# Windowed attention on one core: score tiles of 196 columns, sink keys inside a 68-key block, and no sink path of its own

## The chip, the cores and the metric

The kernel runs on one core of a Trainium2 chip. The core has a matmul engine (TensorE, PE in the tables, with its weight loads as PEld), a vector engine (VectorE, DVE), an activation engine (ScalarE, ACT), a general engine (GpSimd, POOL) and a sync engine that issues transfers (SyncE, SP). Each works through its own list of instructions in order and waits for others by semaphores. The metric is the device time of one launch in microseconds (us), the median of several runs; lower is better.

## The reference

Attention over 2 batches, 8 heads, 768 positions and 64 dimensions per head, with a causal window of 128 keys and 4 sink keys that every query sees; behind it two feed-forward networks without biases, all in float32.

```python
scores = scale * np.matmul(q, k.transpose(0, 1, 3, 2))
is_sink = pos[None, :] < int(n_sink)                 # n_sink 4
rel = pos[:, None] - pos[None, :]
keep = is_sink | ((rel >= 0) & (rel < int(window)))  # window 128
a = np.exp(np.where(keep, scores, -1e9) - rowmax)
x = (a / (a.sum(-1) + 1e-9)) @ v                     # heads side by side: 1536 x 512
x = ((x @ w1) * (x @ w2)) @ w3 @ w_out               # 512 -> 1024 -> 512
h = x @ w_in                                         # 512 -> 2048
out = softplus(h) @ w_out2                           # 2048 -> 512
```

## The kernel before, in words

Attention comes first, then stages 1 and 2 (the first network, with w3 and w_out multiplied ahead), stage 3 and stage 4 (the second network). The weights arrive as 64-bit numbers and are decoded on ACT and DVE; each matmul behind attention is three passes over split operands (`mm3`, L158 to L160). The decoding of the first weights of stage 1 (`D`) is planned among attention's work, that of the later ones is held behind `self.gate`, the last sink copy of attention on ACT (L463).

Attention works on pairs of heads, 8 pairs, each pair on the two halves of the partitions. A pair has six tiles of 128 queries. In a tile, queries are rows and keys are columns: 128 keys of the block before, the 4 sink keys, 128 keys of the own block, 260 in all (the first tile has its own block alone). Its upper 64 query rows need the first 196 columns, its lower 64 the last 196, except in tile 1, whose lower half takes all 260. `score` (L375) thus issues four matmuls a tile, one for each quarter of the array: half of the rows by head. `mask` (L383, DVE) scales, adds a bias and takes the row maximum, `exp` (L390, ACT) exponentiates and sums, `divide` (L404, POOL) scales by the inverse sum. `turn` (L416, PE) transposes the blocks of 128 keys, eleven a head in three groups g of up to four, into one of two PSUM buffers; `turned` copies them to SBUF on DVE (L426) or ACT (L428). `pv` (L451) multiplies with V: the weights are the 64 columns of V of a key block, the moving side is the turned block for the own tile and the tile behind it, so mostly 256 columns; two heads side by side in two column groups, in two PSUM banks.

The sinks of tiles 2 to 5 have a path of their own. `sink_copy` (L434, L435, L143, POOL) gathers their four columns of each tile, in a high and a low part, into a small tile for the pair; `sink_turn` (L460, PE) transposes it, `sink_turned` (L463, ACT) copies it, and `sink_pv` (L470, PE) adds four matmuls with the sink rows of V onto the banks. Those rows come by `sink_load` (L315) and are split by `sink_hi` (L140, POOL) and `sink_values` (L329, DVE). Then `x_hi` (L485, ACT) and `x_lo` (L143, DVE) write x for stage 1.

All steps are given to a planner (`Plan`) with engine, an assumed duration, what they need, and a rank (their place of adding plus an offset from `PUT_OFF`). It emits the steps in one order, which sets each engine's list; `form` adds a cost wherever PE changes its matmul form. 64 matmuls on a zero tile (`heat`, L510) fill PE at the start; four clears of the score banks (L515) are on DVE.

Of the kernel before, what the change touches and what calls it, by code (L numbers as in the profile page):

```python
# [28 lines left out]
KB = P + NSINK  # L29
EW = KB + P  # L30
# [17 lines left out]
    nw=-0.5, iota=-88.6, val=-119.97, inw=-95.56, cur=13.36, snk=-82.32, prev=-13.45, km1=109.48, m_1p=27.86,  # L48
    m_1c=141.05, km0=119.34, m_0=-213.7, m_p=-49.48, m_s=-4.31, m_c=11.17, heat=25.88, clear=(-245.94, -30.95),
    zeros=-0.98, q0=(204.36, 54.81), k0=(66.05, 234.03), v=(-1.12, -22.79), S=(19.74, 17.7), M=(-25.38, 3.94),  # L50
    E=(8.85, 10.07), N=(2.71, 10.01), RC=(-171.36, -209.28), C=(39.62, 36.0), T=(21.68, 18.7),
    P=(-267.36, -54.12), K=(-3.88, 41.33), PV=(21.75, 23.37), vs=-11.44, vsh=(39.09, -30.53),
    vsl=(-166.45, -4.22), KT=(21.93, 2.35), KC=(-167.02, -50.49), KV=(23.63, 24.74), XH=(-199.87, -147.15),
    XL=(1.84, 12.41), qk=(55.63, -83.58), flag=241.29, D=(12.72, 16.36),
)

PVS = ([(0, 0, 2), (1, 0, 2), (2, 0, 2), (3, 0, 1)], [(3, 1, 2), (4, 0, 2), (5, 0, 1)])


class Plan:  # L60
# [70 lines left out]
class Net:  # L131
# [116 lines left out]
    def mask_steps(self, pool):  # L248

        nc = self.nc  # L250
        n, w = self.val[:, 0:1], self.val[:, 1:2]
        rel = pool.tile([P, P], I32, name="rel")
        col = pool.tile([P, P], I32, name="col")
        inw, cur, snk, prev, k0, k1, self.m_0 = (
            pool.tile([P, P], F32, name=x) for x in ("inw", "cur", "snk", "prev", "k0", "k1", "m_0")
        )
        m_1, m_mid = self.m_1, self.m_mid = [pool.tile([P, EW], F32, name=x) for x in ("m_1", "m_mid")]

        def bias(engine, dst, keep):
            engine.tensor_scalar(out=dst, in0=keep, scalar1=-1.0, scalar2=MASKED, op0=ALU.add, op1=ALU.mult)  # L260

        def start():
            nc.gpsimd.iota(rel, pattern=[[-1, P]], base=0, channel_multiplier=1)
            nc.gpsimd.iota(col, pattern=[[1, P]], base=0, channel_multiplier=0)
            nc.gpsimd.memset(m_1[:, P:KB], -MASKED)

        return [
            ("iota", "Pool", 650, start, ()),
            ("val", "DVE", 550, lambda: self.window_values(pool), ()),
            ("inw", "DVE", 196, lambda: nc.vector.tensor_scalar(  # L270
                out=inw, in0=rel, scalar1=w, scalar2=None, op0=ALU.is_lt), ("iota", "val")),
            ("cur", "DVE", 202, lambda: nc.vector.scalar_tensor_tensor(
                out=cur, in0=rel, scalar=0.0, in1=inw, op0=ALU.is_ge, op1=ALU.mult), ("inw",)),
            ("snk", "DVE", 196, lambda: nc.vector.tensor_scalar(
                out=snk, in0=col, scalar1=n, scalar2=None, op0=ALU.is_lt), ("val", "iota")),
            ("prev", "DVE", 196, lambda: nc.vector.tensor_scalar(
                out=prev, in0=rel, scalar1=float(P), scalar2=w, op0=ALU.add, op1=ALU.is_lt), ("val", "iota")),
            ("km1", "DVE", 202, lambda: nc.vector.tensor_tensor(out=k1, in0=prev, in1=snk, op=ALU.max), ("prev", "snk")),
            ("m_1p", "Pool", 268, lambda: bias(nc.gpsimd, m_1[:, 0:P], k1), ("km1",)),
            ("m_1c", "DVE", 135, lambda: bias(nc.vector, m_1[:, KB:EW], cur), ("cur",)),  # L280
            ("km0", "DVE", 202, lambda: nc.vector.tensor_tensor(out=k0, in0=cur, in1=snk, op=ALU.max), ("cur", "snk")),
            ("m_0", "DVE", 135, lambda: bias(nc.vector, self.m_0, k0), ("km0",)),
            ("m_p", "Pool", 268, lambda: bias(nc.gpsimd, m_mid[:, 0:P], prev), ("prev",)),
            ("m_s", "Pool", 164, lambda: bias(nc.gpsimd, m_mid[:, P:KB], snk[:, 0:NSINK]), ("snk",)),
            ("m_c", "ACT", 160, lambda: nc.scalar.copy(m_mid[:, KB:EW], m_1[:, KB:EW]), ("m_1c",)),
        ]
# [14 lines left out]
    def sink_zeros(self, pool):  # L301
        nc = self.nc
        self.skb = []
        for i in range(2):
            t = pool.tile([P, QT - 2, 32], FR, name=f"sk{i}")
            d = pool.tile([P, P], FR, name=f"skd{i}")
            nc.gpsimd.memset(t.bitcast(F32), 0.0)
            self.skb.append((t, d))

    def sink_load(self, pool):  # L310
        self.part = pool.tile([P, 1], F32, name="part")
        self.vsraw = []
        for j in range(2):
            self.vsraw.append(self.ring.tile([P, B * NPAIR, P], F32, tag="u", name=f"vsraw{j}", bufs=5))
            self.nc.sync.dma_start(out=self.vsraw[j], in_=self.vsink[:, j])  # L315
        self.nc.sync.dma_start(out=self.part, in_=self.vpart)
        self.vshi, self.vs = [], []

    def sink_hi(self, pairs, j):
        if len(self.vshi) == j:  # L320
            self.vshi.append(self.ring.tile([P, B * NPAIR, P], FR, tag="u", name=f"vshi{j}", bufs=5))
        self.hi_pool(self.vshi[j][:, pairs], self.vsraw[j][:, pairs])

    def sink_values(self, pool, pairs, j):


        if len(self.vs) == j:
            self.vs.append(pool.tile([P, B * NPAIR, P], FR, name=f"vs{j}"))
        self.nc.vector.scalar_tensor_tensor(  # L329
            out=self.vs[j][:, pairs], in0=self.vshi[j][:, pairs].bitcast(F32), scalar=self.part[:, 0:1],  # L330
            in1=self.vsraw[j][:, pairs],
            op0=ALU.mult, op1=ALU.add,
        )

    def attention(self, pool, psum):
# [5 lines left out]
        shape = dict(qk=[P, S + QT * KB], v=[P, QT, P], e=[P, QT, EW], st=[P, 3, QT], pt=[P, 2 * QT - 1, P])  # L341
# [11 lines left out]
        def load_qk(pair, cuts=((0, S + QT * KB),)):  # L353
            for a, b in cuts:
                nc.sync.dma_start(out=buf("qk", pair)[:, a:b], in_=self.qk[pair][:, a:b])

        def load_v(pair):
            nc.sync.dma_start(out=buf("v", pair), in_=self.v[pair])

        def tile_columns(i):  # L360
            return slice(KB, EW) if i == 0 else slice(0, EW)

        def score(pair, i):

            qk, k = buf("qk", pair), S + (i - 1) * KB
            for par in range(2):
                held["S", 2 * pair + par, i] = banks[2 * (scores.index((pair, i)) % 2) + par]
            for half in range(2):

                rows = slice(half * D, half * D + D)  # L370
                a, b = (0 if i < 2 else D, EW) if half else (0, EW - D)
                a = a if i else KB
                for par in range(2):
                    r = slice(par * D, par * D + D)
                    nc.tensor.matmul(  # L375
                        held["S", 2 * pair + par, i][rows, a:b], qk[r, i * P + half * D : i * P + half * D + D],
                        qk[r, k + a : k + b], start=True, stop=True, skip_group_check=True,
                    )
# [33 lines left out]
        def turn(h, g):  # L412
            held["PT", h, g] = ps = psum.tile([P, 4, P], F32, tag="PT", name=f"ptp{h}_{g}", bufs=2)
# [8 lines left out]
        def turned(h, g):  # L422
            lo, n = max(4 * g - 1, 0), len(blocks(g))
            dst, src = buf("pt", h)[:, lo : lo + n, :], held.pop(("PT", h, g))[:, 0:n, :]
            if on_dve(h, g):
                nc.vector.tensor_copy(dst, src)  # L426
            else:
                nc.scalar.copy(dst, src)  # L428

        def sink_copy(h):  # L430
            sk = self.skb[(h // 2) % 2][0]
            src = buf("e", h)[:, 2:QT, P:KB]
            c = [slice((2 * g + h % 2) * NSINK, (2 * g + h % 2 + 1) * NSINK) for g in range(3)]
# [567 lines left out]
```

## Time and profile before

| what | value |
|---|---|
| runs | 590.69, 593.15, 593.74 us; median 593.15 |
| profiled execution | 593.03 us, span 591.1 us, 8685 instructions |
| busy, share of span | PE 98%, weight loads 79%, DVE 75%, ACT 60%, POOL 15% |
| bytes moved | 52.10 MB, HBM read 48.32, written 3.15 |

The time of an execution is its span, from the first to the last instruction, and some 1.9 us around it. Busy time is a union over an engine's instructions; matmuls are pipelined, so several records of PE overlap, and a busy PE may still be draining. Every fp32 matmul shows as two records and two weight loads. A group is named by its line, so the lines above tell which step it is.

### The profile page before, as it was taken

To read this page: it belongs to the slowest core of one execution; us is meant where nothing else is said; L and a number is where in the kernel's file an instruction comes from. 1 tells how busy PE (TensorE), PEld (TensorE's weight loads), DVE (VectorE), ACT (ScalarE), POOL (GpSimd) and SP (SyncE) were. 2 spreads that over 40 slices of the span, in tenths; PEclk is the share of its full clock that TensorE was granted. 3 is DMA by queue.
4 is the path that set the end of the run, shared out by engine and by line. 5 is a ranking of instruction groups with operands and counts; after the bars stand their busy time and mean duration, and the time that the engine had idled before them with its cause. 6 is when DMAs were issued, how large, how long until landed. Compare 5 with 4: busy or idle time off the path is not lost.

```text
span 591.1 us, 8685 instructions
## 1 busy us (share of the span) xinstructions
PE 579.9 (98%) x3096; PEld 468.1 (79%) x3096; DVE 441.9 (75%) x920; ACT 353.2 (60%) x720; POOL 90.9 (15%) x213
## 2 busy tenths in 40 slices
PE   8899999999999999999999999999999999999996
PEld 6576678888878878888888788888888888888884
DVE  7899969989998987784999799855545544644553
ACT  6899967667666565553566777643543444444352
POOL 3887840000000000000000111101110110111010
PEclk9999999999999999999999999999999999999998
DMA  8853204435453452441545031000100000100002
GB/s 261 302 172 106 63 2 145 160 123 177 145 171 113 144 160 89 142 132 31 165 137 178 2 120 59 0 1 0 73 0 1 1 1 1 71 0 1 1 0 78
DMA packets 15459, 52.10 MB, mean 88 GB/s; under 512 B 1968, under 2 KB 2480, under 8 KB 15408
## 3 DMA queue, kind: packets, MB, share of 16 engines
q1 hardware_dynamic: 15120, 50.95, 26.3%
q8 instruction: 26, 0.43, 0.3%
q10 hardware_dynamic: 288, 0.52, 0.2%
q14 instruction: 25, 0.20, 0.1%
HBM read 48.32 MB, written 3.15 MB: 87 GB/s over the span
## 4 chain that ended last, share of the span: by engine, by line
PE 63%; DVE 7%; ACT 6%; DMA 6%; issue 0%; POOL 0%; ACTq 0%; SPq 0%; DVEq 0%
PE h L160 7%; PE h L158 7%; PE h L159 7%; DMA raw_w<-w3t 4%; PE ox L158 4%; PE ox L160 4%; PE x2p L159 4%; PE x2p L158 4%; PE o L158 4%; PE o L160 4%; PE ox L159 4%; PE o L159 4%; PE x2p L160 4%; PE ab L160 3%; PE ab L159 3%; PE ab L158 3%
## 5 line engine op out<-in xcount | busy, mean ns | idle before, releaser
L736 POOL TENSOR_SCALAR spu<-spa 128x512 f32<-128x512 f32 (+1 forms) x49 | 30.3, 619 | 465.6 <-ACT spa L735 465.6
L143 DVE TENSOR_TENSOR gl<-spl,gh 128x512 fp32r<-128x512 f32 x47 | 32.6, 693 | 77.1 <-ACT gh L750 76.9
L734 ACT ACTIVATE spa<-h 128x512 f32<-128x512 f32 (+1 forms) x49 | 28.8, 588 | 88.8 <-PE h L160 88.6
L160 PE MATMUL ab<-x,u_w 128*128 128x512 f32 x192 | 75.0, 391 | 0.4 <-DVE u_w L143 0.3
L158 PE MATMUL ab<-x,u_w 128*128 128x512 f32 x192 | 75.1, 391 | 0.0
L159 PE MATMUL ab<-x,u_w 128*128 128x512 f32 x192 | 74.7, 389 | 0.0
L158 PE MATMUL h<-y,w4h 128*128 128x512 f32 x192 | 74.7, 389 | 0.0
L160 PE MATMUL h<-y,w4l 128*128 128x512 f32 x192 | 74.7, 389 | 0.0
L159 PE MATMUL h<-y,w4h 128*128 128x512 f32 x192 | 74.7, 389 | 0.0
L184 ACT ACTIVATE dt_w<-raw_w 128x512 bf16<-128x512 bf16 x64 | 42.4, 670 | 49.4 <-DMA raw_w<-w4d 13.8
L192 DVE SCALAR_TENSOR_TENSOR dc_w<-raw_w,dt_w 128x512 uint16<-128x512 uint16 x64 | 43.8, 689 | 14.5 <-ACT dt_w L187 13.4
L404 POOL TENSOR_SCALAR e<-e,st 128x260 f32<-128x260 f32 (+1 forms) x96 | 47.2, 510 | 16.5 <-ACT e L390 8.6
L390 ACT ACTIVATE e<-e,st 128x260 f32<-128x260 f32 (+1 forms) x96 | 46.5, 491 | 2.7 <-DVE st L383 2.5
L741 DVE SCALAR_TENSOR_TENSOR spu<-spu,spa 128x512 f32<-128x512 f32 (+1 forms) x49 | 33.3, 680 | 17.7 <-ACT spl L739 17.6
L187 ACT ACTIVATE dt_w<-dt_w,rebias 128x512 uint16<-128x512 uint16 x64 | 45.8, 722 | 1.2
L160 PEld LDWEIGHTS ab<-x,u_w 128*128 128x128 f32 x192 | 36.0, 188 | 8.6 <-DVE u_w L143 1.3
L158 PEld LDWEIGHTS ab<-x,u_w 128*128 128x128 f32 x192 | 36.1, 188 | 8.0 <-ACT u_w L216 0.6
L160 PEld LDWEIGHTS h<-y,w4l 128*128 128x128 f32 x192 | 36.1, 188 | 7.6
L159 PEld LDWEIGHTS h<-y,w4h 128*128 128x128 f32 x192 | 36.0, 188 | 7.5
L158 PEld LDWEIGHTS h<-y,w4h 128*128 128x128 f32 x192 | 36.0, 188 | 7.4
L159 PEld LDWEIGHTS ab<-x,u_w 128*128 128x128 f32 x192 | 36.0, 188 | 7.3
L739 ACT ACTIVATE spl<-spu 128x512 f32<-128x512 f32 (+1 forms) x49 | 30.4, 623 | 18.8 <-POOL spu L736 18.1
(138 smaller groups left out, 1335.3 us busy)
## 6 DMA issues: line engine op xcount, KB each, us to landing
raw_w<-w4d SPq DMA_DIRECT2D x32, 511.8 KB, 4.1
raw_w<-w SPq DMA_DIRECT2D x16, 511.8 KB, 4.3
raw_w<-w3t SPq DMA_DIRECT2D x16, 511.8 KB, 3.8
qk<-qk SPq DMA_DIRECT2D x7, 780.0 KB, 6.4
raw_wo<-wod SPq DMA_DIRECT2D x8, 511.8 KB, 3.7
v<-v SPq DMA_DIRECT2D x8, 384.0 KB, 5.6
out<-os SPq DMA_DIRECT2D x10, 256.0 KB, 2.3
vsraw<-vsink SPq DMA_DIRECT2D x2, 512.0 KB, 7.9
```

The costliest lines, as they stand in the source:

```text
L143: return engine.tensor_tensor(out=lo, in0=x, in1=hi.bitcast(F32), op=ALU.subtract)
L158: nc.tensor.matmul(ps, lhs[0], rhs[0], start=start, stop=False)
L159: nc.tensor.matmul(ps, lhs[0], rhs[1], start=False, stop=False)
L160: nc.tensor.matmul(ps, lhs[1], rhs[0], start=False, stop=stop)
L184: return nc.scalar.activation(t.bitcast(BF), x["top"].bitcast(BF), AF.Abs)
L187: return nc.scalar.activation(x["t"], x["t"], AF.Relu, bias=self.rebias[:, 0:1], scale=8.0)
L192: nc.vector.scalar_tensor_tensor(out=c, in0=x["top"], scalar=0x8000, in1=t, op0=ALU.bitwise_and, op1=ALU.bitwise_or)
L390: nc.scalar.activation(e, e, AF.Exp, bias=st[:, 0, i : i + 1], scale=-1.0, accum_out=st[:, 1, i : i + 1])
L404: nc.gpsimd.tensor_scalar(out=e, in0=e, scalar1=buf("st", h)[:, 2, i : i + 1], scalar2=1.0, op0=ALU.mult, op1=ALU.mult)
L736: nc.gpsimd.tensor_scalar(out=u[:, c], in0=a[:, c], scalar1=1.0, scalar2=1.0, op0=ALU.add, op1=ALU.mult)
L739: nc.scalar.activation(l[:, c], u[:, c], AF.Ln)
L741: nc.vector.scalar_tensor_tensor(out=u[:, c], in0=u[:, c], scalar=1.0, in1=a[:, c], op0=ALU.subtract, op1=ALU.subtract)
```

## The change

A strip is 64 queries, and keys are kept in blocks of 64, each with the four sink keys ahead of it (68 columns). A tile now has 196 columns: 68 of one single block and 128 of a pair of blocks. For the upper strip the pair is the 128 keys behind and the single block its own; for the lower strip the pair is the tile's own 128 keys and the single block the one two strips back. So each strip sees its 192 keys and the sinks in 196 columns, and every row of the tile uses all of them. `score` issues eight matmuls a tile, four of 68 columns and four of 128. `turn` turns the 68 columns to 68 rows, in which the sinks are the first four. `pv` multiplies the pair's block with V as before, for the strips that use it, and each single block with 68 rows of V, sinks among them, which a second transfer brings (`vu`, ten blocks of 68 rows a pair of heads). The sink path is gone: POOL's copies, the turn, the copy and the product, the load and the splits. The gate is now the last copy of `turned` on ACT. The first 16 of the warm-up matmuls write the banks and the turn buffers, in place of the clears. The masks are built by other steps, and the planner's offsets are new.

```diff
 def load_v(pair):
-    nc.sync.dma_start(out=buf("v", pair), in_=self.v[pair])
+    nc.sync.dma_start(out=buf("v", pair)[:, 0:QT], in_=self.v[pair])
+    nc.sync.dma_start(out=buf("v", pair)[0:KU, QT:], in_=self.vu[pair])
...
 def score(pair, i):
-    for half in range(2):
-        rows = slice(half * D, half * D + D)
-        a, b = (0 if i < 2 else D, EW) if half else (0, EW - D)
-        a = a if i else KB
-        for par in range(2):
-            r = slice(par * D, par * D + D)
-            nc.tensor.matmul(
-                held["S", 2 * pair + par, i][rows, a:b], qk[r, i * P + half * D : i * P + half * D + D],
-                qk[r, k + a : k + b], start=True, stop=True, skip_group_check=True,
-            )
+    for part in range(1 if i else 0, -1, -1):
+        for half in range(2):
+            s, rows = 2 * i + half, slice(half * U, half * U + U)
+            for par in range(2):
+                ...
+                if part:
+                    out, k = out[rows, 0:KU], k[:, s - 2 if half else s]
+                else:
+                    b = i if half or not i else i - 1
+                    out, k = out[rows, KU:EW], k[:, 2 * b : 2 * b + 2, NSINK:]
+                nc.tensor.matmul(
+                    out, qk[r, s * U : s * U + U], k, start=True, stop=True, skip_group_check=True
+                )
...
 def turn(h, g):
-    for j, (t, own) in enumerate(blocks(g)):
-        c = slice(KB, EW) if own else slice(0, P)
-        nc.tensor.transpose(ps[:, j, :], buf("e", h)[:, t, c], self.ident)
+    for j, (t, pair) in enumerate(blocks(g)):
+        n, c = (P, slice(KU, EW)) if pair else (KU, slice(0, KU))
+        nc.tensor.transpose(ps[0:n, j, :], buf("e", h)[:, t, c], self.ident)
...
-PVS = ([(0, 0, 2), (1, 0, 2), (2, 0, 2), (3, 0, 1)], [(3, 1, 2), (4, 0, 2), (5, 0, 1)])
+PVS = (
+    [(0, 0, 1), (0, 1, 3), (1, 3, 5), (2, 5, 7), (3, 7, 8)],
+    [(3, 8, 9), (4, 9, 11), (5, 11, 12)],
+)
...
 def pv(pair, bank):
-    for n, (j, s0, s1) in enumerate(PVS[bank]):
+    todo = [(slice(0, P), v[:, j], s0, s1, 1) for j, s0, s1 in PVS[bank]]
+    todo += [
+        (slice(0, KU), v[0:KU, QT + s - 2], s, s + 1, 0)
+        for s in range(8 if bank else 2, 12 if bank else 8)
+    ]
+    for n, (rows, w, s0, s1, own) in enumerate(todo):
...
-                nc.scalar.copy(dst, src)
+                self.gate = (nc.scalar.copy(dst, src),)
...
-        def sink_copy(h):
-        def sink_turn(pair):
-        def sink_turned(pair):
-        def sink_pv(pair):
```

PE's list, a stretch of the middle pairs, before (s are the scores, ptp the turns, xt the product with V, and with skd and vs the sink product):

```order
L375 MATMUL s_108<-qk_735 64x196
L416 MATMUL ptp_1_1086<-ident,e_850 128x128 x4
L416 MATMUL ptp_2_1094<-ident,e_850 128x128 x4
L470 MATMUL xt_0_1007<-skd_139,vs_437 128x128
L470 MATMUL xt_1_1040<-skd_139,vs_437 128x128
L470 MATMUL xt_0_1007<-skd_139,vs_439 128x128
L470 MATMUL xt_1_1040<-skd_139,vs_439 128x128
L375 MATMUL s_109<-qk_735 64x196
```

The sink product stands between turns and scores, as a form of its own (64 rows by 128 columns of the array). And PE's list after the change, from the end of a product with V on (pt are the turns):

```order
L448 MATMUL xt_1_983<-pt_843,v_605 64x64
L412 MATMUL pt_106<-ident,e_763 128x128
L412 MATMUL pt_106<-ident,e_763 68x128
L412 MATMUL pt_106<-ident,e_763 128x128
L412 MATMUL pt_107<-ident,e_763 68x128
L412 MATMUL pt_107<-ident,e_763 128x128
L412 MATMUL pt_107<-ident,e_763 68x128
L412 MATMUL pt_107<-ident,e_763 128x128
L371 MATMUL s_102<-qk_550 64x68
```

No sink product or turn stands between the others. Over two pairs of heads PE's list before (47.44 to 65.14 us of its trace) has 19 groups of one kind of matmul: three of products with V, seven of scores, seven of turns (a sink turn counted with its neighbours) and two sink products. After, a pair in the middle has seven: turns, scores, turns, scores, turns, scores, product; each score group covers two tiles.

DVE's list at the start, where the masks are built, before (m are the finished masks):

```order
L272 SCALAR_TENSOR_TENSOR cur<-rel,inw 128x128
L278 TENSOR_TENSOR k_102<-prev,snk 128x128
L281 TENSOR_TENSOR k_101<-cur,snk 128x128
L260 TENSOR_SCALAR m_103<-k_101 128x128
L260 TENSOR_SCALAR m_104<-cur 128x128
```

Here the two masks wait for nothing but DVE's own steps. DVE's list at the same place after the change:

```order
L275 SCALAR_TENSOR_TENSOR keep<-rel,inw 128x192
L272 TENSOR_SCALAR inw<-rel,val 128x128
L275 SCALAR_TENSOR_TENSOR keep<-rel,inw 128x128
L290 SCALAR_TENSOR_TENSOR m_100<-keep,bias 64x4
L284 TENSOR_TENSOR keep<-keep 128x4
L287 TENSOR_SCALAR bias<-keep 128x128
L378 ISA e_194,st_195<-s_103,bias 128x128
```

The second tile's mask, m_100, is finished on DVE (L290) from ACT's copy of a bias that POOL makes, and it stands ahead of the first tile's mask (L287) and the first masking (L378).

ACT's list at the end of attention, before (L428 are copies of turns, L463 the sink copy, L184 the first step of decoding):

```order
L428 COPY pt_1319<-ptp_0_1315 128x384
L485 CAST x_2_77<-xt_0_1283 128x256
L485 CAST x_2_81<-xt_0_1283 128x256
L485 CAST x_2_81<-xt_1_1304 128x256
L428 COPY pt_1342<-ptp_0_1338 128x384
L428 COPY pt_1342<-ptp_1_1349 128x512
L463 CAST skd_142<-skp_1385 128x128
L184 ACTIVATE dt_w_1_0_1420<-raw_w_1_0_1418 128x512
```

The first decoding step stands right behind the last sink copy. ACT's list there after the change:

```order
L424 COPY pt_1468<-pt_106 128x384
L424 COPY pt_1468<-pt_107 128x512
L463 CAST x_2_81<-xt_1_1478 128x256
L424 COPY pt_1500<-pt_106 128x384
L184 ACTIVATE dt_w_1_0_1578<-raw_w_1_0_1576 128x512
```

Decoding follows the last copy of a turn instead of the sink copy.

## Rows read from the trace of the kernel before

**Rows 1.** The page: busy us, share and instructions; PE's granted clock in tenths, 40 slices.
```profile
PE 579.9 (98%) x3096; PEld 468.1 (79%) x3096; DVE 441.9 (75%) x920; ACT 353.2 (60%) x720; POOL 90.9 (15%) x213
...
PEclk9999999999999999999999999999999999999998
```
**Rows 2.** Stretches: length, busy of PE, PEld, DVE, ACT, POOL, PE clock, DMA share, GB/s.
```profile
30.00:50.00 20.00, 19.87 (x234) 13.69 (x230) 19.79 (x81) 19.44 (x70) 16.11 (x38) 1.00 0.55 182
...
84.00:591.00 507.00, 500.89 (x2204) 412.83 (x2202) 369.90 (x617) 282.64 (x469) 30.31 (x49) 1.00 0.23 76
```
**Rows 3.** Timeline of PE: start and length in us, engine, line, tiles, form, count.
```profile
44.48 0.56 PE L375 MATMUL s<-qk 64*64 64x196 f32 x8
...
47.44 2.60 PE L451 MATMUL xt<-pt,v 128*64 128x256 f32 x28
...
51.82 0.44 PE L470 MATMUL xt<-skd,vs 64*128 64x128 f32 x4
52.19 0.89 PE L375 MATMUL s<-qk 64*64 64x196 f32 x16
...
60.76 1.09 PE L416 MATMUL ptp<-ident,e 128*128 128x128 f32 x8
61.78 0.44 PE L470 MATMUL xt<-skd,vs 64*128 64x128 f32 x4
...
64.44 0.65 PE L416 MATMUL ptp<-ident,e 128*128 128x128 f32 x4
64.93 0.27 PE L460 MATMUL skp<-ident,sk 128*128 128x128 f32 x1
65.14 0.65 PE L451 MATMUL xt<-pt,v 128*64 128x256 f32 x4
```
**Rows 4.** Timeline of PE's weight loads, with idle time before them and its releaser.
```profile
62.88 0.31 PEld L416 LDWEIGHTS ptp<-ident,e 128*128 128x128 f32 x3 [0.46 <-POOL e L404]
```
**Rows 5.** Waits of PE from 84 us on: us in total, times, longest.
```profile
PE ab L160 <- DVE u_w L143: 0.3, 1, 0.3
```
**Rows 6.** Timeline of PE, 10 to 20 us: the second run of warm-up matmuls.
```profile
11.82 1.18 PE L510 MATMUL heat<-idle 128*128 128x128 bf16 x18
```
**Rows 7.** Groups by line and shape (three of 30 to 84 us, one of 0 to 120): busy, mean ns.
```profile
L390 ACT ACTIVATE e<-e,st 128x260 f32<-128x260 f32 x51 | 25.7, 511 | 1.8 <-DVE st L383 1.8
L383 DVE CUSTOM_DVE_ANT_0 e<-s,m_mid 128x260 f32<-128x260 f32 x40 | 15.4, 416 | 0.1
...
L390 ACT ACTIVATE e<-e,st 128x128 f32<-128x128 f32 x10 | 4.0, 400 | 0.0
...
L383 DVE CUSTOM_DVE_ANT_0 e<-s,m 128x128 f32<-128x128 f32 x10 | 2.7, 274 | 0.0
...
L329 DVE SCALAR_TENSOR_TENSOR vs<-vshi,part,vsraw 128x384 fp32r<-128x384 f32 x4 | 2.7, 712 | 0.0
```
**Rows 8.** Timeline of ACT: the first decoding step, and the last sink copy.
```profile
24.23 0.69 ACT L184 ACTIVATE dt_w<-raw_w 128x512 bf16<-128x512 bf16 x1 [1.81 <-DMA raw_w<-w]
...
82.46 0.27 ACT L463 CAST skd<-skp 128x128 fp32r<-128x128 f32 x1 [2.73 <-PE skp L460]
```
**Rows 9.** Waits of PE, 12 to 30 us.
```profile
PE ptp L416 <- ACT pt L428: 1.4, 1, 1.4
```
**Rows 10.** Transfers by issue: queue, count, KB each, median us to landing.
```profile
qk<-qk SPq DMA_DIRECT2D x7, 780.0 KB, 6.4
...
v<-v SPq DMA_DIRECT2D x8, 384.0 KB, 5.6
...
vsraw<-vsink SPq DMA_DIRECT2D x2, 512.0 KB, 7.9
```
**Rows 11.** Timeline of all engines at the first masks.
```profile
4.04 0.67 POOL L260 TENSOR_SCALAR m_mid<-prev 128x128 f32<-128x128 f32 x1 [1.95 <-DVE prev L276]
...
5.63 0.29 DVE L383 CUSTOM_DVE_ANT_0 e<-s,m 128x128 f32<-128x128 f32 x1 [0.69 <-PE s L375]
```
**Rows 12.** Timeline of PE at the end of attention.
```profile
83.69 0.50 PE L158 MATMUL ab<-x,u_w 128*128 128x512 f32 x1
```

More of the change, by code (lines that the diff above doesn't have):

```diff
@@ L76, in form @@
     def form(s):
-        return {"S": "quarters", "KV": "rows", "PV": "columns"}.get(s["key"][0], "whole")
+        return {"S": "quarters", "PV": "columns"}.get(s["key"][0], "whole")
     def __init__(self, rings):
@@ new lines, in mask_steps, with behind @@
+        self.m_1 = pool.tile([P, EW], F32, name="m_1")
+        self.m_mid, self.m_0 = bias[:, 0:EW], bias[:, EW:]
+        snk, first = keep[:, 0:NSINK], keep[:, EW : EW + NSINK]
+        def start():
+            nc.gpsimd.iota(rel[:, EW - NSINK :], pattern=[[-1, P]], base=0, channel_multiplier=1)
+            nc.gpsimd.iota(col, pattern=[[1, NSINK]], base=0, channel_multiplier=0)
+        def behind():
+            for half, (own, pair) in enumerate(((0, 2 * U), (2 * U, U))):
+                r = slice(half * U, half * U + U)
+                nc.gpsimd.iota(rel[r, 0:U], pattern=[[-1, U]], base=own, channel_multiplier=1)
+                nc.gpsimd.iota(rel[r, U : EW - NSINK], pattern=[[-1, P]], base=pair, channel_multiplier=1)
@@ new lines, in inside, with kept, sinks, added @@
+        def inside(c):
+            nc.vector.tensor_scalar(out=inw[:, c], in0=rel[:, c], scalar1=w, scalar2=None, op0=ALU.is_lt)
+        def kept(c):
+            nc.vector.scalar_tensor_tensor(
+                out=keep[:, c.start + NSINK : c.stop + NSINK], in0=rel[:, c], scalar=0.0, in1=inw[:, c],
+                op0=ALU.is_ge, op1=ALU.mult,
+            )
+        def sinks():
+            nc.vector.tensor_scalar(out=snk, in0=col, scalar1=n, scalar2=None, op0=ALU.is_lt)
+        def added():
+            nc.vector.tensor_tensor(out=first, in0=first, in1=snk, op=ALU.max)
@@ L267, in mask_steps, with biased, second @@
+        def biased(engine, c):
+            engine.tensor_scalar(out=bias[:, c], in0=keep[:, c], scalar1=-1.0, scalar2=MASKED, op0=ALU.add, op1=ALU.mult)
+        def second():
+            nc.vector.scalar_tensor_tensor(
+                out=self.m_1[0:U, KU : KU + NSINK], in0=snk[0:U], scalar=-MASKED, in1=self.m_mid[0:U, KU : KU + NSINK],
+                op0=ALU.mult, op1=ALU.add,
+            )
+        mid, own = slice(0, EW - NSINK), slice(EW - NSINK, EW - NSINK + P)
         return [
-            ("iota", "Pool", 650, start, ()),
+            ("iota", "Pool", 500, start, ()),
+            ("iotb", "Pool", 900, behind, ()),
@@ L282, in mask_steps @@
[L282 to L285, printed above, removed]
+            ("inw", "DVE", 196, lambda: inside(own), ("iota", "val")),
+            ("cur", "DVE", 202, lambda: kept(own), ("inw",)),
@@ new lines, in mask_steps @@
+            ("snk", "DVE", 80, sinks, ("val", "iota")),
+            ("km0", "DVE", 80, added, ("cur", "snk")),
+            ("m_0", "DVE", 135, lambda: biased(nc.vector, slice(EW, EW + P)), ("km0",)),
+            ("inb", "DVE", 264, lambda: inside(mid), ("iotb", "val")),
+            ("prev", "DVE", 270, lambda: kept(mid), ("inb",)),
+            ("m_p", "Pool", 410, lambda: biased(nc.gpsimd, slice(0, EW)), ("prev", "snk")),
+            ("m_c", "ACT", 210, lambda: nc.scalar.copy(self.m_1, self.m_mid), ("m_p",)),
@@ L286, in mask_steps @@
+            ("m_1", "DVE", 80, second, ("m_c",)),
         ]
@@ L507, in attention, with warm @@
         heat = psum.tile([P, CH], F32, tag="X0", name="heat", bufs=1)
+        banks = [psum.tile([P, EW], F32, tag="S", name=f"s{i}", bufs=4) for i in range(4)]
+        held["turns"] = [psum.tile([P, 4, P], F32, tag="PT", name=f"pt{i}", bufs=2) for i in range(2)]
+        clear = [x for i in range(4) for x in (banks[i][:, 0:P], banks[i][:, P:EW])]
+        clear += [x[:, j, :] for x in held["turns"] for j in range(4)]
+        heats = clear + [heat[:, 0:P]] * (64 - len(clear))
+        def warm(i):
+            nc.tensor.matmul(heats[i], self.idle, self.idle[:, 0 : heats[i].shape[-1]], start=True, stop=True)
         for i in range(64):
             add(
-                "heat", "PE", 54, lambda i: nc.tensor.matmul(heat[:, 0:P], self.idle, self.idle, start=True, stop=True),
-                i, after=() if i < 44 else [("M", 0, 5)],
-            )
-        banks = [psum.tile([P, EW], F32, tag="S", name=f"s{i}", bufs=4) for i in range(4)]
-        for i in range(4):
-            add("clear", "DVE", 330, lambda i: nc.vector.memset(banks[i], 0.0), i)
-        add("zeros", "Pool", 1200, lambda: self.sink_zeros(pool))
+                "heat", "PE", 54, warm, i, after=() if i < 44 else [("M", 0, 5)],
+            )
         for j in range(2):
```

185 lines of the change are left out of this document (51 added, 134 removed).

## The prediction, made before the changed kernel ran

> **What bounds the kernel now.** [...] A busy PE need not be the bound, since PE counts as busy while a matmul drains; so next come the stretches [rows 2]. From 84 us on PE is busy 500.9 of 507 us: there the stages behind attention stream 512-column matmuls, which the change doesn't touch. The change lives in the first 84 us, where all engines are nearly full: from 30 to 50 us PE is busy 19.87, VectorE (DVE) 19.79, ScalarE (ACT) 19.44 and GpSimd (POOL) 16.11 of 20 us [rows 2]. Which sets the pace is seen in PE's list over two pairs of heads, 47.44 to 65.14 us [rows 3]: each group starts as the one before it drains. Only once in this stretch is the load row idle for longer than at every change of matmul form: 0.46 us at 62.88, for POOL [rows 4]. After 84 us PE's waits sum to 0.3 us [rows 5]. So from about 30 us on attention runs at the pace of PE's own list, 17.70 us for two pairs, and what leaves this list moves the end, as far as the other engines follow.
>
> **PE's prices** [rows 3]. Every fp32 matmul runs as two passes. A score group of two 196-column tiles (x16) lasts 0.89 us, one of a single such tile (x8) 0.56; a tile is thus 0.33: two passes of 196 columns with the four quadrants at once, 0.84 ns a column. Turns: x8 lasts 1.09, x4 0.65, so a 128-column step costs 0.11, with its own 128-column weight load inside it. The product with V (x28, 2.60 us) is 14 steps, two heads side by side: 1408 columns a head, twice, at 0.84 are 2.37, the rest is start and drain. A group has a fixed price: from 60.76 to 61.78 eight turns take 1.02, of which 8 x 0.109 is 0.87, so 0.15.
>
> **The change, per pair of heads.**
> - Sink product (L470): 51.82 to 52.19, -0.37, its change of form included.
> - Sink turn (L460): 64.93 to 65.14 where the form changes behind it, 0.21, and one step, 0.11, where more turns follow: -0.17.
> - Other groups: two pairs hold 19, two of them sink products. In the new order the same work repeats seven groups a pair: turns, scores of two tiles, turns, two tiles, turns, two tiles of which one is the narrow first, product. That is 14 for two pairs where 17 stood: three fewer at 0.15, -0.23 a pair.
> - Scores: 196 columns as 68 and 128. The one tile with 260 columns on a half now has 196: 64 x 2 x 0.84, -0.11. Five tiles get two more starts at about 3 ns (0.109 less 128 x 0.84 is 2): +0.03.
> - Product with V: the columns stay, the steps grow from 14 to 36, of which 28 have 64 columns. No row shows a long run of 64-column steps. From below such a step costs its columns, 0.054; from above as much as a 128-column step, 0.109. Nearest is the idle warm-up: 18 bf16 matmuls, each with a weight load of its own, in 1.18 us [rows 6]; less some 0.23 for the last one's latency that is 0.056 a step. I take 0.057, with 22 more starts: +0.08. The upper end adds 28 x 0.052 = 1.46, and ten 68-column waves of the scores another 0.5.
>
> Sum: -0.37 - 0.17 - 0.23 - 0.08 + 0.08 = **-0.77 us a pair**.
>
> [...]
>
> **Do the others follow?** Per pair DVE runs ten masks of 260 columns at 416 ns, against 274 for 128 [rows 7]: 1.08 ns a column, 64 columns fewer, -0.69. ACT: 511 against 400, ten times 0.054, and a sink copy of 0.27 goes [rows 8]: -0.8, as much as PE. POOL had 3.9 of 20 us to spare [rows 2] and loses 64 columns of each division and six sink copies. DVE shrinks by 0.08 less than PE, and in its fullest 20 us it had 0.21 to spare, where the decoding of the next stage's weights lies beside attention. It should just follow; I count no gain beyond PE's.
>
> **The start** is not PE's. ACT stands still for 1.81 us until 24.23, waiting for the first weights of the next stage [rows 8], and PE then waits 1.4 us for ACT's copy [rows 9]. The bytes ahead of these weights hardly change: four query-key loads of 780 KB, three V loads of 384 and the sink values, 1024, are 5296 KB [rows 10]; now 792 KB each, 384 + 340 (68 rows of 5 KB), no sink values: 5340. SP issues two DMAs for each V load, and the second V load now stands ahead of the fourth query-key load; three sink issues go. The first masks lose: on DVE the second tile's mask (L290) waits for ACT's copy of POOL's bias, and the first tile's mask and all that follows is queued behind it. The first masking starts at 5.63 now [rows 11]; POOL's bias took 0.67 for 128 columns, and a copy and two handovers lie behind it, so I expect about 6. ACT still reaches the weights earlier, by some twenty exponentials at 0.054, and then waits longer. Of the first two pairs' 1.54 us I count half, with none and all as ends. DVE and POOL also lose the splits of the sink values (six each; DVE's took 0.71 us for 384 columns [rows 7]) and the clearing of banks and buffers, which 16 of the warm-up matmuls take over. All of it lies before 31 us, where ACT's stall and PE's wait for ACT cover it: I count nothing, and the full gain of the start, the upper end, is what it could be worth.
>
> **The tail.** Four matmuls of the next stage ran between the last turns; two do now. Each is 0.23 us (507 us for 2204 [rows 2]): +0.45. Behind attention PE's list is the same row for row. Decoding of the next weights was released by the last sink copy, at 82.46 [rows 8]; now by ACT's last turn copy, ahead of the last product, so it should lead PE by more.
>
> Sum: six pairs at -0.77 are -4.6, the start -0.77, the tail +0.45: **-4.9 us**. The profiled execution took 593.03 us (span 591.1 and 1.9 around it), the median of the runs 593.15. Predicted: 588.1 us.
>
> **Rivals.**
> 1. *Narrow steps don't hide their loads: slower.* A 64- or 68-column step costs what a 128-column one does: 38 x 0.052 = +1.98 us a pair, net +1.21; times 8, +0.45: 603 us. It decides from 20 ns a step on (0.77 / 38), a step of 0.075. For it: no long run of 64-column steps has a row. Against: turns and warm-up hide loads that are as long as their streams. [...] Chance 0.07.
> 2. *More than forecast.* The start gains in full and the shorter chain from exponential to turn takes PE's wait of 1.4 [rows 9] and half of the 0.46 per two pairs [rows 4] with it: 6.2 + 1.4 + 0.9 - 0.45 = 8.0, with steps at 0.054 another 0.9: 584.1. Against: the weights' landing, which holds ACT, doesn't move. Chance 0.18.
> 3. *The gain is swallowed.* The start gains nothing and its stall grows; or DVE sets the pace; or decoding, which holds PE for 0.3 us at one place now [rows 5], doesn't move as far as PE and holds it longer. Each leaves 1 to 3 of the 4.9: 590 to 592. Chance 0.15.
> 4. That the sink path stays in part can't be: the new list has no line of it.
>
> **How the numbers follow.** The forecast, 586 to 590, has 0.60. The range, 584.1 to 592.0, leaves out rival 1 and the tails. A measurement of this kernel can tell about 0.5% from no change, 590.1 to 596.0: most of rival 3 lies there. Faster 0.80, same 0.13, slower 0.07.
>
> **What would show it.** A whole pair's product (x72) in 2.6 to 2.75 us, where rival 1 has over 4; two-tile score groups (x32) at 0.9; two pairs in 16.2 us; no sink rows; the unbroken stage starting near 78.8 instead of 83.69 [rows 12], and all behind it earlier by as much. If pairs take 16.2 and the end doesn't move, the loss is at ACT's first weights or at PE's waits behind attention.

## The result, and the profile after

The changed kernel takes 600.26 us (median of 4 runs, 598.59 to 601.18), the kernel before 592.88 (4 runs, 590.69 to 593.74): 1.0127 times the time, interval 1.0089 to 1.0165. Slower by 7.4 us, where 4.9 us less were forecast. The page of the changed kernel, beside [rows 1]: TensorE's busy share by slices, its granted clock, the DMA engines' busy share, and what they moved.

```profile
PE   7559999999999999999999999999999999999996
...
PEclk9959999999999999999999999999999999999999
DMA  8927504444453543341446023000100000100002
GB/s 244 265 104 224 162 26 141 142 142 142 145 173 107 160 139 124 107 129 48 146 137 193 19 74 104 0 1 0 71 0 2 1 1 1 71 0 1 0 1 77
```

The loss is in the second and third slice, 15 to 45 us: TensorE is half idle, and in the third the clock falls to half. From there to the last slice TensorE is full, as before. The stretches, by engine (columns as in [rows 2]):

```profile
12.00:24.00 12.00, 11.38 (x245) 9.45 (x242) 9.40 (x49) 9.69 (x40) 9.39 (x24) 1.00 1.02 250
24.00:32.00 8.00, 0.19 (x8) 0.00 (x0) 1.27 (x9) 0.00 (x0) 0.00 (x0) 0.77 0.78 229
32.00:40.00 8.00, 2.91 (x32) 2.39 (x32) 1.64 (x5) 4.08 (x14) 0.00 (x0) 0.50 0.25 100
```

The last two columns are the DMA engines' share and GB/s. From 12 to 24 us the DMA engines are full but move 250 GB/s; from 32 to 40 they are busy to 0.25, four of sixteen, while ACT stands until 35.92 and TensorE until 37.09. The kernel before, same view:

```profile
12.00:24.00 12.00, 11.69 (x139) 7.96 (x136) 11.00 (x46) 9.82 (x39) 11.50 (x29) 1.00 0.99 365
```

What waits is ACT, for the first weights of the next stage, as in [rows 8], but 14.24 us in place of 1.81; TensorE waits for ACT's copy, 12.90 in place of the 1.4 of [rows 9]. The timelines of ACT and of PE, and one row of the chain of waits:

```profile
21.19 0.40 ACT L385 ACTIVATE e<-e,st 128x128 f32<-128x128 f32 x1
21.49 0.19 ACT L385 ACTIVATION_READ_ACCUMULATOR e<-e,st 128x1 f32 x1
35.92 0.65 ACT L184 ACTIVATE dt_w<-raw_w 128x512 bf16<-128x512 bf16 x1 [14.24 <-DMA raw_w<-w]
```

```profile
23.29 0.90 PE L371 MATMUL s<-qk 64*64 64x68 f32 x32
37.09 1.89 PE L412 MATMUL pt<-ident,e 128*68 128x128 f32 x8 [12.90 <-ACT pt L424]
38.91 1.36 PE L371 MATMUL s<-qk 64*64 64x128 f32 x24
40.20 4.41 PE L448 MATMUL xt<-pt,v 128*64 128x64 f32 x100
...
49.75 2.73 PE L448 MATMUL xt<-pt,v 128*64 128x64 f32 x72
...
65.80 2.73 PE L448 MATMUL xt<-pt,v 128*64 128x64 f32 x72
...
89.96 0.50 PE L158 MATMUL ab<-x,u_w 128*128 128x512 f32 x1
```

```profile
12.36 23.54 DMA raw_w<-w
```

The weights were issued at 12.36 us and were 23.54 us on their way. Behind the stall attention runs as forecast: whole products (x72) in 2.73 where [rows 3] has 2.60, two pairs of heads from 49.75 to 65.80, 16.05 us, where 16.2 were forecast and 17.70 are in [rows 3]. The unbroken stage starts at 89.96, not at 83.69 [rows 12].

Which packets are in flight when is in the trace's DMA packets. The load of the second part of V (`vu`, 68 rows of 5 KB) is the only one with packets of 5120 bytes: once its first rows have started, up to four at a time run (four from 12.75 to 16, from 19.25 to 22.25 and from 30.5 to 31.75 us; five or six only for a moment, at 22.5). From 32 to 40 us four data packets at a time run in all, of whatever load.

### The profile page after: what moved, and what is told of

Same layout as the page of the kernel before. It is cut to its first block, busy times and chain, and to the rows that moved or that the text cites. A ratio compares the mean times of both kernels' runs of the same rounds, so it can differ in the third digit from the quotient of the medians.

```text
span 596.0 us, 9861 instructions
## 1 busy us (share of the span) xinstructions
PE 573.9 (96%) x3728; PEld 475.3 (80%) x3728; DVE 432.7 (73%) x910; ACT 347.8 (58%) x712; POOL 73.7 (12%) x158
## 4 chain that ended last, share of the span: by engine, by line
PE 92%; DMA 5%; ACT 1%; SPq 0%; issue 0%; DVE 0%; POOL 0%
PE ab L158 7%; PE ab L160 7%; PE ab L159 7%; PE h L160 7%; PE h L158 7%; PE h L159 7%; DMA raw_w<-w 4%; PE ox L158 4%; PE ox L160 4%; PE o L158 4%; PE x2p L160 4%; PE ox L159 4%; PE o L159 4%; PE x2p L158 4%; PE o L160 4%; PE x2p L159 4%
## 5 line engine op out<-in xcount | busy, mean ns | idle before, releaser
L697 POOL TENSOR_SCALAR spu<-spa 128x512 f32<-128x512 f32 (+1 forms) x49 | 30.5, 622 | 465.7 <-ACT spa L696 465.7
L184 ACT ACTIVATE dt_w<-raw_w 128x512 bf16<-128x512 bf16 x64 | 42.3, 669 | 62.3 <-DMA raw_w<-w 19.0
L399 POOL TENSOR_SCALAR e<-e,st 128x196 f32<-128x196 f32 (+1 forms) x96 | 41.1, 449 | 40.6 <-DVE st L395 31.3
L385 ACT ACTIVATE e<-e,st 128x196 f32<-128x196 f32 (+1 forms) x96 | 42.2, 445 | 2.8 <-DVE st L378 2.4
```

The source lines that it names most:

```text
L184: return nc.scalar.activation(t.bitcast(BF), x["top"].bitcast(BF), AF.Abs)
L385: nc.scalar.activation(e, e, AF.Exp, bias=st[:, 0, i : i + 1], scale=-1.0, accum_out=st[:, 1, i : i + 1])
L399: nc.gpsimd.tensor_scalar(out=e, in0=e, scalar1=buf("st", h)[:, 2, i : i + 1], scalar2=1.0, op0=ALU.mult, op1=ALU.mult)
L697: nc.gpsimd.tensor_scalar(out=u[:, c], in0=a[:, c], scalar1=1.0, scalar2=1.0, op0=ALU.add, op1=ALU.mult)
```

## The experiments

Theory A was formed on that: a load of 68 rows is cut among four of the sixteen DMA engines, and what is queued behind it on these four, the first weights among it, comes late. Rivals: B, it is the bytes and the order of the loads; C, it is the narrow steps. In these kernels the lines of the file stand a few further down than in the two that they are made from.

**80 rows, and 64 + 4 rows.** In the first, `vu` gets twelve rows of zeros; in the second the same 68 rows go as two loads.

```
-            nc.sync.dma_start(out=buf("v", pair)[0:KU, QT:], in_=self.vu[pair])
+            nc.sync.dma_start(out=buf("v", pair)[0:80, QT:], in_=self.vu[pair])
...
+            for a, b in ((0, 64), (64, 68)):
+                nc.sync.dma_start(out=buf("v", pair)[a:b, QT:], in_=self.vu[pair][a:b])
```

> The second part of V is loaded as 80 rows of 5 KB in place of 68; rows 68 to 79 are zeros that nothing reads. Theory A (four engines): from 31 to 41 us only four of the sixteen DMA engines had packets in the changed kernel, and all packets of 5120 bytes ran four at a time; a transfer of 68 rows is cut among 4 engines, 17 rows each, and every later transfer, the first weights among them, waits for these four. 80 rows go to 16 engines, 5 each. Then the first weights land about 25 us in place of 35.9, ACT's wait there falls from 14.2 to about 3, the granted clock stays at the upper level, the unbroken stage starts near 78.5 in place of 90, and the time is 587 to 590 us. Theory B (bytes and order): the second part of V stands ahead of the weights and its bytes hold them; then 60 KB more per load make it no better: 599 to 602 us. Theory C (narrow steps): the loss is in the 64-column steps; nothing changes, 599 to 601 us.

> The second part of V is loaded as two transfers, 64 rows and 4 rows, without any more bytes. Theory A: 64 rows go to 16 engines, 4 each; the 4 rows put one row of 5 KB on each of four engines, 0.2 to 0.3 us, so the first weights land as early as with 80 rows, within 0.5 us, or a little earlier for 60 KB less per load; one more issue of 0.33 us on SP for each pair. Time 587 to 590 us. Theory B: same bytes and same order as the changed kernel: 599 to 602 us.

Measured: 80 rows 591.32 us, 1.0004 of the kernel before (0.9986 to 1.0022); 64 + 4 rows 592.28, 1.0012 (0.9997 to 1.0027). B and C fall: more bytes in the same order, and the same steps, are as fast as the kernel before, where the changed one has 1.0127. But both miss A's 587 to 590. With 80 rows the weights landed at 27.5, not 25, and with 64 + 4 rows at 28.5, later still; ACT waited, and the granted clock, expected to stay at the upper level, was 0.50 from 28 to 34 us. ACT's line with 80 rows:

```profile
27.48 0.65 ACT L187 ACTIVATE dt_w<-raw_w 128x512 bf16<-128x512 bf16 x1 [6.18 <-DMA raw_w<-w]
```

All sixteen engines are now busy (share 1.05 and 1.04), and still they move little, 241 and 240 GB/s (stretches of this kernel, last columns as above):

```profile
12.00:18.00 6.00, 6.00 (x128) 4.88 (x127) 4.79 (x25) 6.00 (x26) 5.06 (x14) 1.00 1.05 241
20.00:26.00 6.00, 3.19 (x74) 2.30 (x72) 3.72 (x18) 1.30 (x5) 2.31 (x6) 1.00 1.04 240
```

**The kernel before with V in 68 + 60 rows.** The narrow tiles are left out of this test altogether.

```
-            nc.sync.dma_start(out=buf("v", pair), in_=self.v[pair])
+            for a, b in ((0, 68), (68, P)):
+                nc.sync.dma_start(out=buf("v", pair)[a:b], in_=self.v[pair][a:b])
```

> The kernel before, with each load of V (128 rows of 3 KB) cut into 68 and 60 rows; nothing else is changed, the bytes and their order stay. Theory A: 68 rows go to 4 engines, 17 each, and 60 rows to 15 engines, 4 each, so four engines get 21 rows, 64.5 KB, where 24.6 KB would be their share; three V loads stand ahead of the first weights: 3 x 40 KB at about 21 bytes a ns is 5.7 us. The first weights land about 30 in place of 24.2, and the time is 596 to 600 us. Theory B: no byte is added, 592 to 594 us.

Measured: 599.80 us, 1.0133 (1.0098 to 1.0168); the weights are first touched at 30.29 us. Landing and time are as A has them, in a kernel that has nothing of the change but a load of 68 rows; B falls. Among how many engines the 60 rows went, no view shows; A's fifteen were an assumption. The way there is only in part A's. ACT, GpSimd and TensorE:

```profile
30.29 0.66 ACT L184 ACTIVATE dt_w<-raw_w 128x512 bf16<-128x512 bf16 x1 [3.58 <-DMA raw_w<-w]
```

```profile
20.55 0.40 POOL L140 TENSOR_SCALAR vshi<-vsraw 128x256 fp32r<-128x256 f32 x1 [2.23 <-DMA vsraw<-vsink]
```

```profile
24.75 0.33 PE L417 MATMUL ptp<-ident,e 128*128 128x128 f32 x1 [2.96 <-POOL e L405]
33.20 1.09 PE L417 MATMUL ptp<-ident,e 128*128 128x128 f32 x4 [1.08 <-ACT pt L429]
```

ACT's wait for the weights cost TensorE 1.08 us. Its longest wait, 2.96, was for GpSimd, which had stood for the sink values, a load that the changed kernel doesn't have; behind that wait the granted clock was 0.50 from 26 to 38 us. So the run shows that a load of 68 rows alone delays others, not by which waits the changed kernel lost its time. That both kernels end 1.3% longer is chance: the changed one's loads cost more (12.1 us, below), and its tiles give some of it back.

**74 rows.**

> The second part of V is loaded as 74 rows, fewer bytes than with 80 rows. Theory A, with the number of engines as the largest one up to 16 that divides the rows: 74 rows go to 2 engines, 37 each; two at a time run, and 3 x (37 - 4.6) rows of 5 KB at 16 to 20 bytes a ns put 25 to 31 us on these two engines ahead of the first weights: they land at 50 to 56 us, and the time is 612 to 625 us. If the division only had to be nearly even (5 rows on most engines), it would be as with 80 rows, 587 to 590 us. Theory B: between the changed kernel and the one with 80 rows in bytes, so 599 to 602 us.

Measured: 620.72 us, 1.0496 (1.0449 to 1.0543), 2 runs; ACT waited 19.37 us until 43.75, not until 50 to 56: once the two engines are alone, a row of 5120 bytes takes 199 ns, 26 bytes a ns, where I had 16 to 20. The time is in A's range all the same, since TensorE waited for later loads too, 4.31 us at one place. Two of sixteen are 0.125, and the stretch shows it (stretch, ACT, PE):

```profile
36.00:49.00 13.00, 4.08 (x46) 3.36 (x48) 2.66 (x12) 4.73 (x17) 0.99 (x3) 0.50 0.15 56
```

```profile
43.75 0.65 ACT L187 ACTIVATE dt_w<-raw_w 128x512 bf16<-128x512 bf16 x1 [19.37 <-DMA raw_w<-w]
```

```profile
44.91 1.89 PE L415 MATMUL pt<-ident,e 128*68 128x128 f32 x8 [18.15 <-ACT pt L427]
76.95 1.36 PE L374 MATMUL s<-qk 64*64 64x128 f32 x24 [4.31 <-DMA qk<-qk]
```

80, 74 and 68 rows gave 16, 2 and 4 engines, by the busy shares of 1.05, 0.15 and 0.25 in the stretches above: in these three cases the largest number up to sixteen that divides the rows.

**Second flaw: which partitions.** Left to explain is why 80 rows are slow with all engines at work. Padded to 128 rows, without another change:

```
+    vu = np.concatenate([vu, np.zeros((B * NPAIR, 128 - KU, NU - 2, P), vu.dtype)], axis=1)
...
-            nc.sync.dma_start(out=buf("v", pair)[0:KU, QT:], in_=self.vu[pair])
+            nc.sync.dma_start(out=buf("v", pair)[:, QT:], in_=self.vu[pair])
```

> With 80 rows all sixteen engines worked, yet from 12 to 18 and from 20.5 to 26 us every packet, those of the query-key loads and of the weights too, took 1.7 times its time: 240 GB/s, against 400 before and after; the slow stretches are those in which rows of the second part of V are in flight. Here this part is padded to 128 rows (640 KB in place of 400), 8 rows for each engine, as in all other loads. Theory P (partitions): a transfer that covers less than the whole of the 128 partitions piles its engines up on a part of the way into SBUF and holds all others; with 128 rows the stretch from 12 to 26 us moves 380 to 410 GB/s. The bytes ahead of the first weights are 6240 KB in place of 5520; at 400 the weights land at 26 to 27 us, where they landed at 27.4: ACT's wait is 4.5 to 6, the time 588.5 to 592 us. Theory Q (size of the rows or the place in HBM makes it slow): 5 KB rows stay slow, 240 GB/s, the weights land at 30 to 31 us, and the time is 594 to 597 us.

Measured: 586.14 us, 0.9923 (0.9899 to 0.9948): faster than the kernel before, with 300 KB more for each pair than the change as it stood. P's rate comes out (413 GB/s where 380 to 410 were given) and Q falls; the weights came at 24.2 and the time at 586.14, both below what I gave. Why the rows matter is a question of its own, below. Stretch, ACT, PE:

```profile
12.00:24.00 12.00, 10.95 (x242) 9.01 (x238) 10.47 (x55) 9.38 (x38) 9.22 (x24) 1.00 1.02 413
```

```profile
24.22 0.65 ACT L187 ACTIVATE dt_w<-raw_w 128x512 bf16<-128x512 bf16 x1 [2.84 <-DMA raw_w<-w]
```

```profile
25.39 1.03 PE L415 MATMUL pt<-ident,e 128*68 128x128 f32 x8 [2.44 <-ACT pt L427]
26.35 0.79 PE L374 MATMUL s<-qk 64*64 64x128 f32 x24
27.07 3.79 PE L451 MATMUL xt<-pt,v 128*64 128x64 f32 x100
...
76.77 0.50 PE L161 MATMUL ab<-x,u_w 128*128 128x512 f32 x1
```

**The kernel before with V in halves, and in even and odd rows; 96 rows.** Two ways to cut 128 rows into 64 and 64:

```
+            for a, b in ((0, 64), (64, P)):
+                nc.sync.dma_start(out=buf("v", pair)[a:b], in_=self.v[pair][a:b])
...
+            for a in range(2):
+                nc.sync.dma_start(out=buf("v", pair)[a:P:2], in_=self.v[pair][a:P:2])
```

> The kernel before, with each load of V cut into rows 0 to 63 and 64 to 127: both halves go to 16 engines, 4 rows each, no byte is added and no engine has more than another. Theory P: each half covers half of the partitions and is slow by itself: packets of all kinds stretch by 1.5 to 1.7 while V is in flight, 1152 KB of V ahead of the weights cost 2 to 4 us more, and the first weights land at 26 to 28 in place of 24.2: 594 to 597 us. Theory Q, or that only an uneven share of the engines matters: as before, 590.5 to 593 us.

> [...] Theory P (what part of the partitions a transfer reaches): packets keep their 121 to 160 ns, the first weights land at 24 to 25, and the time is 591 to 593 us. Rival (two half transfers are slow for any choice of rows): as with the halves, 594 to 597 us.

> 96 rows in the second part of V, 6 for each of sixteen engines: 480 KB, less than 128 rows, more than 80. If full speed needs that each engine writes its own 8 rows out of 128, 96 rows are slow as 80 were, 240 to 260 GB/s, and the time is 590 to 593 us. If reaching all of the ways into SBUF is enough, and 96 rows do, it is as fast as with 128 rows or a little faster for 160 KB less: 585 to 587 us. Between both: 587 to 590 us, slow only in part.

Measured: halves 595.89 us, 1.0084 (1.0056 to 1.0112); even and odd rows 591.02, 1.0008 (0.9988 to 1.0028); 96 rows 594.13, 1.0044 (1.0018 to 1.0069). Loads of 64 rows, with the same bytes and issues, cost 5 us or nothing, by which rows they are; with the halves too the engines were full, with a share of 1.06 from 20 to 26 us. With 96 rows 480 KB are slower than 640 KB with 128: reaching more partitions wasn't enough. The time is even above the 590 to 593 of the slow case: ACT waited 7.58 us, until 28.34, and the granted clock was 0.50 from 22 to 35 us, both more than with 80 rows. Stretches of this kernel:

```profile
12.00:18.00 6.00, 6.00 (x128) 4.99 (x122) 4.93 (x27) 6.00 (x26) 5.21 (x14) 1.00 1.03 237
20.00:26.00 6.00, 3.60 (x50) 2.73 (x49) 1.88 (x10) 0.76 (x3) 1.78 (x5) 0.65 1.03 265
22.00:35.00 13.00, 10.05 (x130) 8.17 (x131) 5.96 (x29) 5.09 (x19) 2.39 (x6) 0.50 0.79 265
```

The time of the halves is P's, but not by the weights, for which ACT waited 0.96 us until 25.69: as with 68 + 60 rows, TensorE waited for GpSimd, 2.21 us at 22.77, and the granted clock was 0.50 from 23 to 32 us.

The median packet from 12 to 26 us, in ns, by its bytes (3072 are V, 4094 the weights, 5120 the second part of V, 6240 or 6336 query and key):

```
                                3072   4094   5120   6240 or 6336
kernel before                    121    159      -    238
changed kernel, 68 rows          174    222    359    434
  80 rows                        205    287    347    399
  96 rows                        191    256    334    376
  128 rows                       121    162    196    241
before, V in halves              208    260      -    285
before, V in even and odd rows   121    159      -    238
```

Where V comes in blocks of fewer than 128 neighbouring rows, the packets of the loads in flight beside it stretch too, those of the untouched query-key loads (285 to 434 ns, against 238 and 241) and weights (222 to 287, against 159 and 162); with even and odd rows none does. What P gives as the cause is not shown: which engine writes which rows, and by what way, is not in the traces. Shown is that the choice of the rows decides: with the same 64 rows a load, V's packets took 208 ns in halves and 121 in even and odd rows.

**Later decoding.** The remaining wait for the weights, taken out of ACT's line by a later place in the plan:

```
+                        need = need + [("PV", 2, 0)] if k == 1 else need
                         add("D", engine, ns, lambda j, k, emit=emit: emit(), j, k, after=need)
```

> 80 rows, and the planner is told that ACT's first decoding instruction of each first weight half comes behind the first product of the third pair of heads; loads stay where they are. If what is left of the loss with 80 rows is only ACT's place in line (6.2 us until 27.5, in which TensorE first has work, then stands for 3.9 us and then runs its next 5 us at half clock), then ACT's wait goes, TensorE's wait with it, the granted clock stays at the upper level, and the unbroken stage starts at 74 to 77 in place of 82.7: 583 to 586 us. If the data of the attention itself (V and query-key loads) are as late as the weights, the wait only moves to TensorE, and the time is 588 to 592 us.

> The kernel before with the same later place of ACT's first decoding. ACT's 1.81 us there and TensorE's 1.4 us behind it are all there is to win: 589 to 592 us. Against the run with 80 rows and late decoding this shows what the narrower tiles are worth when neither kernel waits for its first weights: by my sum 0.77 us for each of eight pairs, less 0.45, 5.7 us. If the narrower tiles were worth nothing, both would end within 1.5 us.

Measured: with 80 rows 591.20 us, 1.0002 (0.9979 to 1.0024), and the kernel before 596.86, 1.0108 (1.0084 to 1.0131). The first is the second case that I gave: ACT's wait for the weights is gone, but TensorE stood for scores instead, and the granted clock was 0.72 from 20 to 26 us:

```profile
22.08 1.36 PE L374 MATMUL s<-qk 64*64 64x128 f32 x23 [1.81 <-issue]
```

The kernel before misses its 589 to 592. Put later, the decoding falls into the stretch in which all engines are nearly full [rows 2], and TensorE, busy 17.87 of 18 us from 30 to 48 and 17.78 from 48 to 66 without the later place, now is:

```profile
30.00:48.00 18.00, 16.52 (x194) 10.97 (x190) 14.87 (x68) 16.43 (x58) 12.48 (x36) 1.00 0.44 147
48.00:66.00 18.00, 15.36 (x173) 9.80 (x174) 16.82 (x69) 15.87 (x57) 13.42 (x31) 1.00 0.25 83
```

The two runs are 5.7 us apart, the figure that I gave for the tiles. That is luck: the later place cost one kernel over 1% and the other nothing.

**Earlier weights.** The other way to the same wait: the first half of the weights is loaded ahead of the third V load.

```
-            first = {0: [("qk", 2)], 1: [("v", 0)], 2: [("qk", 3)]}
+            first = {0: [("qk", 2)], 1: [("v", 0)], 2: [("D", 0, 0)]}
```

> 128 rows as before, and the first half of the first weights is loaded ahead of the third V load (384 and 640 KB) in place of behind it. With 128 rows ACT still waited 2.84 us for these weights and TensorE 2.44 us for ACT. 1024 KB at 400 GB/s are 2.5 us: the weights land at 21.7, as ACT reaches them; the third V load is needed at 27 us and lands at about 24.5. Theory: both waits go, 583 to 585 us. Rival: TensorE next waits for something else in the same place (scores of the fourth pair of heads, masks), 585 to 587 us.

> The kernel before with the same exchange: the first half of the first weights ahead of the third V load (384 KB, 0.9 us). ACT's wait of 1.81 us falls to about 0.9; at most 1 us comes of it: 590 to 592 us. Together with the run of 128 rows and the same exchange this prices the narrow tiles without their start: 5 to 6.5 us between the two if my sum of 0.77 us a pair holds.

Measured: with 128 rows 585.13 us, 0.9896 (0.9875 to 0.9916), the lowest median of the study, though not clear of 128 rows alone (0.9899 to 0.9948); the kernel before 590.64, 0.9987 (0.9973 to 1.0001), no change clear of the noise, though its waits of [rows 8] for the weights and of [rows 9] are gone. With 128 rows ACT's wait fell to 0.29 us at 21.42. Part of the rival came true: TensorE then stood 1.02 us inside the second pair's product, for nothing that the profile names (ACT, PE):

```profile
21.42 0.69 ACT L187 ACTIVATE dt_w<-raw_w 128x512 bf16<-128x512 bf16 x1 [0.29 <-DMA raw_w<-w]
```

```profile
26.61 2.61 PE L451 MATMUL xt<-pt,v 128*64 128x128 f32 x68 [1.02 <-issue]
```

PE's products, first with 128 rows, then in the kernel before, both with earlier weights:

```profile
35.23 2.73 PE L451 MATMUL xt<-pt,v 128*64 128x64 f32 x72
...
51.23 2.73 PE L451 MATMUL xt<-pt,v 128*64 128x64 f32 x72
...
75.39 0.50 PE L161 MATMUL ab<-x,u_w 128*128 128x512 f32 x1
```

```profile
46.01 2.60 PE L451 MATMUL xt<-pt,v 128*64 128x256 f32 x28
...
63.71 2.60 PE L451 MATMUL xt<-pt,v 128*64 128x256 f32 x28
...
82.28 0.50 PE L158 MATMUL ab<-x,u_w 128*128 128x512 f32 x1
```

Two pairs take 16.00 and 17.70: the narrow tiles are worth 0.85 us a pair, and the two medians are 5.5 us apart, where 5 to 6.5 were expected.

## Why the prediction was wrong

**The step that failed** is in "The start": "The bytes ahead of these weights hardly change", 5296 to 5340 KB. The bytes were right and were the wrong measure. I wrote down that the second V load has 68 rows of 5 KB, and took only its bytes into the sum. Four engines took the 68 rows (busy share 0.25 from 32 to 40 us), in three such loads ahead of the weights, and the packets of the loads beside them stretched meanwhile (6336 bytes in 434 ns in place of 241). The weights came at 35.9 in place of 24.2, and where the sum has -0.77 for the start, the form of the load cost some 12 us. The stall was the one that the prediction named as its sign ("at ACT's first weights"), but rival 3 ("its stall grows") let it leave 1 to 3 of the 4.9 us and named nothing that could make a load of the same bytes slower.

The account, changed kernel against 128 rows, which differ in this load alone: the unbroken stage starts at 89.96 and 76.77, 13.2 apart. TensorE's wait for ACT is 12.90 against 2.44, 10.5; the groups behind it ran at half clock, wholly or in part, 1.89 + 1.36 + 4.41 against 1.03 + 0.79 + 3.79, 2.05; ahead of it scores stood 0.62, for nothing that the profile names. That is 13.1. Against the kernel before, timed beside each, the steps are 1.0127, 1.0004 with 80 rows and 0.9923 with 128: of 591 us that is 7.3 us between 68 rows, on four engines, and 80, on sixteen, and 4.8 between 80 rows and 128, on sixteen engines both: 12.1.

**The other steps, point by point.**
- Sum of a pair, -0.77: held. Two pairs in 16.05 (changed) and 16.00 (earlier weights) against 17.70, -0.83 and -0.85.
- 64-column steps at 0.057, product +0.08: held; a product lasts 2.73 against 2.60, +0.13 with its drain. Rival 1, narrow steps that don't hide their loads, would have over 4 and is out. The slower result has rival 1's sign and size (603 us) by another cause; by the time alone one would have taken it for right.
- Scores: two tiles (x32) 0.90 against the forecast 0.9.
- First masks, forecast at about 6: the first came at 6.95, since the first scores waited 1.34 us for their query-key load. It cost nothing that can be found: the first product starts at 17.83, before at 18.22.
- Tail, +0.45: two matmuls of the next stage between the last turns, as read from the order.
- Behind attention TensorE's list is as before; both kernels pass there without a wait over half a us.
- The 1.9 us around the span, taken over unchanged: wrong. In the runs of the kernel before they are 1.75 to 1.95; in the changed kernel 2.6 to 2.9 (598.59 against a span of 596.0), with 128 rows 2.4 to 2.9 (586.14 against 583.3). Some 0.9 us is lost there, outside of what the profile shows; with 64 + 4 rows, and with 80 rows and late decoding, it isn't (1.9 and 1.8). The cause stays open.
- The sum itself: with the load mended the kernel takes 0.9923 of the time before (0.9899 to 0.9948); 588.1 against 593.15 is 0.9915. The tiles do what was worked out, and the load that feeds them undid it. That the total comes so close is in part luck: the start gained nothing even so (ACT waits 2.84 us in place of 1.81, TensorE 2.44 in place of 1.4) and 0.9 went around the span, while a pair gave somewhat more than 0.77. The span alone is 6.0 us shorter (medians 583.3 and 589.3).

## What to carry to other kernels

When a change alters the shape of a load, count its rows, not only its bytes: here 68 rows ran on four DMA engines and 74 on two, and the first weights queued behind them were touched at 35.92 and 43.75 us, where 128 rows had 24.22. Zeros that fill a load up to 128 rows can be cheaper than leaving them out: 640 KB beat 340, 400 and 480 KB here (586.14 us against 600.26, 591.32 and 594.13). And a stall at the start of a chain of loads is not cured by moving its consumer into a stretch where the engines are full: in the kernel before that cost 1.1%. An earlier load cost nothing there; what it gained with 128 rows isn't clear of the noise.

## What the runs showed of the hardware

Beside loads of a block of fewer than 128 rows, other loads took longer in these kernels: packets of 6336 bytes took 434 ns beside the 68-row load, 399 beside 80 rows, 376 beside 96 and 241 beside 128, though they came from a load that was the same in all four; 64 even or odd rows slowed nothing (3072 bytes in 121 ns, as before). Once only four engines had work, from 32 to 40 us, their packets of 5120 bytes took 199 ns, about what they take with 128 rows (196). TensorE's granted clock fell from 1.00 to 0.50 in the long stall, at 28.25 us, and stayed there until 41.90, for the first 4.8 us of work behind it; with 128 rows it stayed at 1.00 from 20 to 30 us, about the wait of 2.44 us, yet with 80 rows and late decoding it fell about a wait of 1.81 us (0.72 from 20 to 26).
